# Uneven halves for dilated attention heads: 96 and 48 positions of a residue instead of 72 and 72

## The chip, the cores and the metric

The kernel runs on one core of one Trainium2 chip. The metric is device time in microseconds of one execution, the median of several runs. The core's engines are PE (matrix multiplication), DVE (vector), ACT (scalar and exponentials), POOL, and SP, which here issues the DMAs.

## The reference

Sliding-window attention feeds a two-layer feed-forward network (FFN) with GELU. Half of the heads have a plain window of 32 positions, the other half a window of 32 positions taken four apart (dilated). All data is float32.

```python
batch, n_heads, seq, head_dim = 8, 8, 576, 64
window, dilation = 32, 4
scores = q @ k.T / sqrt(64)
rel = pos[:, None] - pos[None, :]
mask_plain = (rel >= 0) & (rel < window)                                   # heads 0..3
mask_dil = (rel >= 0) & (rel < window * dilation) & (rel % dilation == 0)  # heads 4..7
attn = softmax(where(mask, scores, -1e9))
x = (attn @ v), heads side by side, reshaped to (8 * 576, 512)
h = x @ w_in                       # 512 -> 2048
out = gelu(h) @ w_out              # 2048 -> 512
```

A dilated query sees only keys whose position leaves the same remainder on division by 4. So a dilated head is four separate sequences ("residues") of 576 / 4 = 144 positions, each with a plain window of 32.

## The kernel before, in words

**Halves.** The 8 batches of 576 positions are cut into 16 half sequences `c` of 288 positions: `c = 2 * batch + half`. The FFN of one half works on tiles of 128 x 288. The eight heads are four pairs `p`: pairs 0 and 1 are plain, pairs 2 and 3 dilated.

**Blocks.** Attention is computed in blocks of 32 queries against 64 keys (the block's own 32 and the 32 before). In a dilated pair a half has 4 residues of 72 positions, so each residue needs three blocks `u`: two full ones and one with 8 positions. The four residues lie side by side on the 128 partitions (32 each). In a plain pair the nine blocks of a half are spread over the four partition groups, with the ninth alone.

**Steps of one pair.**
- `load` brings q and k (`raw_qk`) by DMA, issued by SP; `all_v` brings v for the four pairs.
- `scores` (line 310): for each block, each residue and each of two heads one matmul of 64 x 32 by 64 x 64 into PSUM.
- `lowest` (line 322): DVE adds the mask and finds the minimum of the negated scores; `softmax` (line 331): ACT's exponential with the sum, one for each block and head.
- `norm` (lines 352 to 361) and `turn` (lines 371 and 376): DVE divides by the sum and transposes the probabilities.
- `av` (line 411): for each block, residue and head one matmul of 64 x 64 by 64 x 32 (by 64 x 8 in a dilated third block) into PSUM tile `px_a`. A float32 matmul is two instructions in the trace, as with the scores.
- `xout` (lines 431 and 434): ACT rounds the result to `xh`, DVE subtracts to get the remainder `xl`. Both feed the FFN. For a dilated pair the store is strided, since positions of the four residues alternate.

**FFN.** Each product is made of three products of rounded parts (high x high, low x high, high x low). `ffn_h` (line 445) makes 12 matmuls for each of 16 tiles `f` of the hidden layer, ACT and DVE make `g` out of it, `ffn_o` (line 459) makes 12 more for each `f`.

**Order.** The halves 0 to 2 and the conversion of the weights are put in order by a planner, class `Plan`: a greedy list scheduler with a cost for each step, ranks, and rings of buffers that a job takes and gives back. The ring `wo` has 18 slots: weights as loaded (`raw_w`, and for some a shifted copy `mid_w`), q, k and v of halves 0 and 1, and the 16 finished `wout` tiles, which stay. The ring `raw` has 5 slots: `raw_qk` from half 2 on, and `cv`, a temporary of the weight conversion. From half 3 on the order is written out by hand: the attention of half `c` is woven into the FFN of half `c - 1`, which has positions 0 to 31 (16 for `ffn_h`, 16 for `ffn_o`).

```python
A_LOAD, A_V, A_SC, A_X = -6, 2, (3, 3, 9, 9), (22.5, 22.5, 27, 27)
```

So the dilated pairs' scores come at position 9, their `av` and `xout` at 27, and the loads six positions before the FFN of half `c - 1` begins.

Of the kernel before, what the change touches and what calls it, by code (L numbers as in the profile page):

```python
# [7 lines left out]
F32 = mybir.dt.float32  # L8
# [6 lines left out]
B, H, S, D = 8, 8, 576, 64  # L15
WIN, DIL = 32, 4
DM, DFF = H * D, 2048
P = 128
HALF = S // 2
NCH = B * 2  # L20
NPAIR = H // 2
NF = DFF // P
NC = DM // P
KW = HALF + WIN
QD = HALF // DIL

KB, NU = 32, 3
QP = HALF // 3  # L30
KD = QD + KB
NKMAX = 3 * KD + (NU + 1) * KB
NEG = -1.0e30
SCALE = 1.0 / 8.0
# [97 lines left out]


@with_exitstack
def attn_ffn(ctx: ExitStack, tc: tile.TileContext, qk_p, qk_d, v_p0, v_d0, v_p, v_d, w_in, w_out, outT):
    nc = tc.nc
    const = ctx.enter_context(tc.tile_pool(name="const", bufs=1))
    wpool = ctx.enter_context(tc.tile_pool(name="wpool", bufs=1))
    wo = ctx.enter_context(tc.tile_pool(name="wo", bufs=NF + 2))
    gpool = ctx.enter_context(tc.tile_pool(name="gpool", bufs=NF + 2))  # L140
    xpool = ctx.enter_context(tc.tile_pool(name="xpool", bufs=NC))
    work = ctx.enter_context(tc.tile_pool(name="work", bufs=2))
# [5 lines left out]
    def upper_banks(name, bufs):  # L148

        upper.close()  # L150
        return upper.enter_context(tc.tile_pool(name=name, bufs=bufs, space=bass.MemoryType.PSUM))
# [17 lines left out]
    select(DILATED0, ANY, None, -KB, 1, 0, ALU.is_ge)  # L169

    pools = dict(px=upper_banks("ps_x", 1))
    wins = [wpool.tile([P, 2, DM], F32R, name=f"win{f}") for f in range(NF)]
    wouts = [None] * NF

# [65 lines left out]
    def new_pair(c, p):  # L240
        s = Pair()
        s.c, s.p = c, p
        s.plain = p < NPAIR // 2
        k = p if s.plain else p - NPAIR // 2
        s.nr, s.nq = (3, QP) if s.plain else (DIL, QD)
        s.across = s.plain and c > 2
        if s.across:
            s.nr, s.nine = 4, 2 * (p % 2)
        s.rows = 32 * s.nr
        s.n = HALF + (KW if s.plain else NKMAX)  # L250
        s.src = (qk_p if s.plain else qk_d)[c, k]
        s.vsrc = (v_p0 if s.plain else v_d0)[c, k] if c < 2 else (v_p if s.plain else v_d)[c - 2, k]
        return s

    def load(s):

        yield {"DMA": 1.0 if s.plain else 1.2}
        if s.c < 2:
            s.raw = wo.tile([P, HALF + NKMAX], F32, tag="wo", name="raw_qk")
        else:  # L260
            s.raw = work.tile([P, HALF + NKMAX], F32, tag="raw", name="raw_qk", bufs=5)
        nc.sync.dma_start(s.raw[:, 0:s.n], s.src)

    def load_v(s):
# [13 lines left out]
    def groups(s, u):  # L278
        return range(s.nine, s.nine + 1) if s.across and u == NU - 1 else range(s.nr)

    def rows_of(s, u):
        g = groups(s, u)
        return slice(32 * g[0], 32 * g[-1] + 32)

    def parts(s):

        return [(rows_of(s, 0), 0, 2), (rows_of(s, 2), 2, 3)] if s.across else [(slice(0, s.rows), 0, NU)]

    def mask_of(s, u):
        k = ANY if s.c % 2 or u else PLAIN0 if s.plain else DILATED0  # L290
# [2 lines left out]
    def scores(s, banks=None):  # L293

        yield {"PE": 0.75}
        if banks is None:
            s.sc = [ps_m.tile([P, 512], F32, tag="m", name="ps_sc")[:, 0:2 * KB * NU] for _ in range(2)]
        else:
            s.sc = [banks[:, h, s.p % 2 * 2 * KB * NU:(s.p % 2 + 1) * 2 * KB * NU] for h in range(2)]
        for u in range(NU):  # L300
            for r in groups(s, u):
                if s.across:
                    q0 = (4 * u + r if u < 2 else 8) * KB
                    k0 = HALF + q0
                else:
                    q0 = r * s.nq + u * KB
                    k0 = HALF + r * (QP if s.plain else KD) + u * KB
                for h in range(2):
                    x = s.raw[h * D:(h + 1) * D]
                    nc.tensor.matmul(s.sc[h][32 * r:32 * r + 32, u * 2 * KB:(u + 1) * 2 * KB], x[:, q0:q0 + 32],  # L310
                                     x[:, k0:k0 + 2 * KB], start=True, stop=True)
# [67 lines left out]
    def av(s, banks=None):  # L379

        yield {"PE": (1.0 if s.plain else 1.3) if s.c < 2 else 0.9}
        n = s.nq
        if s.c < 2:
            px = pools["px"].tile([P, 4, 512], F32, tag="px", name="px")
            s.px = [(px[:, 0:s.nr, 0:n], 0, s.nr)]

            for m in (1, 3, 0, 2):
                i0, k = (2 * (m - 1) * 2 + 1, 2) if 0 < m < NU else (0, 1) if m == 0 else (4 * (NU - 1) + 1, 1)
                q0 = max(m - 1, 0) * KB
                for r in range(s.nr):  # L390
                    rows = slice(32 * r, 32 * r + 32)
                    t = s.t[rows].rearrange("p i j b -> p (i j) b")
                    for h in range(2):
                        i = i0 + 2 * h
                        nc.tensor.matmul(px[h * D:(h + 1) * D, r, q0:q0 + k * KB], s.v[rows, m, h * D:(h + 1) * D],  # L395
                                         t[:, i:i + 3 * k - 2:3], start=m == 1, stop=m == 2)
            return
        if banks is None:
            px = [ps_m.tile([P, 512], F32, tag="m", name="px2").rearrange("p (a n) -> p a n", a=2) for _ in range(2)]
            s.px = [(px[0][:, :, 0:n], 0, 2), (px[1][:, 0:s.nr - 2, 0:n], 2, s.nr)]  # L400
        else:
            at = s.p % 2 * QP
            s.px = [(banks.rearrange("p k (a n) -> p (k a) n", a=2)[:, 0:s.nr, at:at + n], 0, s.nr)]
        for u in range(NU):
            b = min(KB, n - u * KB)
            for j in range(2):
                for r in sorted((r for r in groups(s, u) if r % 2 == j), reverse=s.across and s.nine > 0):
                    px, r0, _ = s.px[-1] if r >= s.px[-1][1] else s.px[0]
                    rows = slice(r // 2 * 64, r // 2 * 64 + 64)
                    for h in range(2):  # L410
                        nc.tensor.matmul(px[h * D:(h + 1) * D, r - r0, u * KB:u * KB + b],  # L411
                                         s.v[rows, u, j, h * D:(h + 1) * D], s.t[rows, 2 * u + h, j, 0:b],
                                         start=True, stop=True)

    def xout(s):
        for i, (px, r0, r1) in enumerate(s.px):
            yield {"ACT": 0.46 if len(s.px) == 1 else 0.34}
            if i == 0:
                if s.c == 1:
                    s.x = s.of["x"][:, s.p, 0], s.of["x"][:, s.p, 1]  # L420
                else:
                    s.x = tuple(xpool.tile([P, HALF], F32R, tag=n, name=n) for n in ("xh", "xl"))
            if s.across:
                two = [x[:, 0:8 * KB].rearrange("p (u r b) -> p r u b", u=2, r=4) for x in s.x]
                put = [(px[:, :, 0:2 * KB].rearrange("p r (u b) -> p r u b", u=2), two),
                       (px[:, s.nine, 2 * KB:], [x[:, 8 * KB:] for x in s.x])]
            else:
                put = [(px, [x.rearrange("p (r i) -> p r i" if s.plain else "p (i r) -> p r i", r=s.nr)[:, r0:r1]
                             for x in s.x])]
            for y, (h, l) in put:  # L430
                nc.scalar.copy(h, y)  # L431
            yield {"DVE": 0.48 if len(s.px) == 1 else 0.3}
            for y, (h, l) in put:
                nc.vector.tensor_sub(l, y, h)  # L434
# [66 lines left out]
    def attention_jobs(plan, c, prev, gate):  # L501

        for p in range(NPAIR):
            s, k, rank = xs[c][p], (c, p), R_ATT[c] + R_P * p

            def add(name, gen, after, take=(), give=(), delay=0.15):
                plan.add((name,) + k, gen, after, take, give, rank + R_A[name], delay)
            last, ring = [] if prev is None else [prev], "wo" if c < 2 else "raw"
            add("load", load(s), [("begun", ("load",) + j) for j in last], [ring], delay=2.2)
            v = ("v",) + k if c < 2 else ("v", c)  # L510
            if c < 2:
# [28 lines left out]
            prev = k  # L540
# [22 lines left out]
    k = attention_jobs(plan, 0, None, [])  # L563
    k = attention_jobs(plan, 1, k, [])
# [54 lines left out]
    for c in range(3, NCH):  # L619
        def add(at, rank, gen, c=c):  # L620
            steps.append((2 * NF * (c - 1) + at, rank, len(steps), gen))
        add(A_V, 0, all_v(c))
        for p, s in enumerate(xs[c]):
            add(A_LOAD, 0, load(s))
            add(A_SC[p], 1, scores_of(s))
            for u in range(NU):
                add(A_SC[p], 2, lowest(s, u))
                add(A_E[p], 3, softmax(s, u))
            add(A_N[p], 4, norm(s))
            add(A_N[p], 5, turn(s))  # L630
            add(A_X[p], 6, av_of(s))
            add(A_X[p], 7, xout(s))
# [98 lines left out]
```

## Time and profile before

| | us |
|---|---|
| timed runs | 948.16, 945.34, 947.63 |
| median of the three | 947.63 |
| profiled execution, its own time | 945.82 |
| span of its trace, first to last instruction | 944.0 |
| PE busy in the span | 916.4 (97%) |
| DVE busy | 500.2 (53%) |
| ACT busy | 435.4 (46%) |
| POOL busy | 21.0 (2%) |

PE and PEld are two rows of one engine: matmuls, and the loads of their stationary operand, which overlap them. The ends of matmuls are modelled in the trace, their starts are recorded. "L445" is line 445 of the kernel. In the chain of work that ended last, each piece is a stretch of one engine's work that the next piece waited for or followed.

### The profile page before, as it was taken

To read this page: it belongs to the slowest core of one execution; us is meant where nothing else is said; L and a number is where in the kernel's file an instruction comes from. 1 tells how busy PE (TensorE), PEld (TensorE's weight loads), DVE (VectorE), ACT (ScalarE), POOL (GpSimd) and SP (SyncE) were. 2 spreads that over 40 slices of the span, in tenths; PEclk is the share of its full clock that TensorE was granted. 3 is DMA by queue.
4 is the path that set the end of the run, shared out by engine and by line. 5 is a ranking of instruction groups with operands and counts; after the bars stand their busy time and mean duration, and the time that the engine had idled before them with its cause. 6 is when DMAs were issued, how large, how long until landed. Compare 5 with 4: busy or idle time off the path is not lost.

```text
span 944.0 us, 27638 instructions
## 1 busy us (share of the span) xinstructions
PE 916.4 (97%) x11632; PEld 898.6 (95%) x11632; DVE 500.2 (53%) x1957; ACT 435.4 (46%) x1398; POOL 21.0 (2%) x64
## 2 busy tenths in 40 slices
PE   4599999999999999999999999999999999999998
PEld 3499999999999999999999999999999999999998
DVE  6889974364635446354454635446354454635420
ACT  5535453634536245363634546255363634546240
POOL 1400020000000000000000000000000000000000
PEclk9999999999999999999999999999999999999999
DMA  9987233022040401204022040401204022040000
GB/s 319 405 297 261 92 126 137 4 78 75 8 145 8 132 17 51 103 8 145 2 82 71 8 146 8 138 9 60 93 8 145 2 86 68 13 139 8 21 1 26
DMA packets 34988, 83.69 MB, mean 89 GB/s; under 512 B 3888, under 2 KB 12080, under 8 KB 34864
## 3 DMA queue, kind: packets, MB, share of 16 engines
q1 hardware_dynamic: 34864, 81.93, 25.3%
q8 instruction: 91, 1.49, 0.7%
q14 instruction: 33, 0.27, 0.1%
HBM read 72.47 MB, written 9.44 MB: 87 GB/s over the span
## 4 chain that ended last, share of the span: by engine, by line
PE 96%; DMA 1%; issue 1%; DVE 1%; ACT 0%; SPq 0%
PE ps_h L445 44%; PE ps_o L459 44%; PE px_a L411 4%; PE ps_a L310 3%; DMA raw_qk<-qk_d 1%; PE px L395 1%; PE ps_sc L310 1%; DMA raw_w<-w_in 0%; DVE sm L322 0%; PE px L411 0%; DVE cv L199 0%; DVE sm L361 0%; ACT sm L331 0%; DVE cv L197 0%; DVE win L232 0%
## 5 line engine op out<-in xcount | busy, mean ns | idle before, releaser
L459 PE MATMUL ps_o<-g,wout 128*128 128x288 f32 x3072 | 420.1, 296 | 0.0
L459 PEld LDWEIGHTS ps_o<-g,wout 128*128 128x128 f32 x3072 | 409.7, 188 | 0.9
L445 PE MATMUL ps_h<-xh,win 128*128 128x288 f32 x1920 | 388.7, 297 | 0.0
L445 PEld LDWEIGHTS ps_h<-xh,win 128*128 128x128 f32 x1920 | 308.2, 188 | 2.8
L445 PE MATMUL ps_h<-xl,win 128*128 128x288 f32 x960 | 284.0, 296 | 0.0
L454 DVE TENSOR_TENSOR g<-gf,g 128x288 fp32r<-128x288 f32 x256 | 117.0, 457 | 259.2 <-ACT g L452 259.0
L449 ACT ACTIVATE gf<-ps_h 128x288 f32<-128x288 f32 x256 | 105.2, 411 | 297.6 <-PE ps_h L445 297.5
L445 PEld LDWEIGHTS ps_h<-xl,win 128*128 128x128 f32 x960 | 181.0, 189 | 0.0
L331 ACT ACTIVATE sm<-sm,st 128x64 f32<-128x64 f32 (+1 forms) x360 | 120.2, 335 | 12.5 <-DVE st L322 11.4
L452 ACT CAST g<-gf 128x288 fp32r<-128x288 f32 x256 | 111.0, 434 | 7.9
L431 ACT CAST xh<-px_a 128x256 fp32r<-128x256 f32 (+1 forms) x78 | 29.5, 413 | 132.7 <-PE px_a L411 84.8
L376 DVE STREAM_TRANSPOSE turned<-sm 32x192 f32<-32x192 f32 (+2 forms) x248 | 81.3, 328 | 6.2
L179 DVE COPY o_sb<-ps_o 128x288 f32<-128x288 f32 x58 | 26.4, 456 | 83.3 <-PE ps_o L459 82.4
L331 ACT ACTIVATION_READ_ACCUMULATOR sm<-sm,st 128x1 f32 (+1 forms) x360 | 67.2, 187 | 0.0
L434 DVE TENSOR_TENSOR xl<-px_a,xh 128x256 fp32r<-128x256 f32 (+1 forms) x78 | 31.3, 429 | 37.5 <-ACT xh L431 37.1
L322 DVE CUSTOM_DVE_ANT_0 sm<-ps_a,masks 128x64 f32<-128x64 f32 (+1 forms) x312 | 48.0, 216 | 0.6
L371 DVE STREAM_TRANSPOSE turned<-sm 128x256 f32<-128x256 f32 (+2 forms) x90 | 41.1, 457 | 9.0 <-POOL sm L358 4.2
L411 PEld LDWEIGHTS px_a<-turned,v_all 64*64 64x64 f32 x2184 | 35.6, 135 | 4.3 <-issue 4.3
L411 PE MATMUL px_a<-turned,v_all 64*64 64x32 f32 (+1 forms) x2184 | 38.2, 216 | 0.0
L361 DVE TENSOR_TENSOR sm<-sm,st 128x256 f32<-128x256 f32 (+2 forms) x82 | 35.1, 428 | 2.8
L352 DVE TENSOR_SCALAR st<-st 128x4 f32<-128x4 f32 (+2 forms) x90 | 14.2, 160 | 31.0 <-ACT sm L331 30.1
L310 PE MATMUL ps_sc<-raw_qk 64*32 64x64 f32 x504 | 12.3, 294 | 18.8 <-issue 8.4
(40 smaller groups left out, 392.8 us busy)
## 6 DMA issues: line engine op xcount, KB each, us to landing
raw_qk<-qk_d SPq DMA_DIRECT2D x32, 364.0 KB, 5.4
v_all<-v_p SPq DMA_DIRECT2D x28, 384.0 KB, 3.8
v_all<-v_d SPq DMA_DIRECT2D x28, 384.0 KB, 5.4
raw_qk<-qk_p SPq DMA_DIRECT2D x32, 304.0 KB, 4.2
outT<-o_sb SPq DMA_DIRECT2D x64, 144.0 KB, 1.8
raw_w<-w_in SPq DMA_DIRECT2D x16, 512.0 KB, 6.1
raw_w<-w_out SPq DMA_DIRECT2D x16, 512.0 KB, 5.7
mid_w<-w_out SPq DMA_DIRECT2D x10, 511.5 KB, 8.0
```

What stands on the lines that cost most here:

```text
L310: nc.tensor.matmul(s.sc[h][32 * r:32 * r + 32, u * 2 * KB:(u + 1) * 2 * KB], x[:, q0:q0 + 32], x[:, k0:k0 + 2 * KB], start=True, stop=True)
L322: nc.vector.tensor_tensor_reduce(out=s.sm[rs, i], in0=s.sc[h][rs, cols], in1=mask_of(s, u), scale=-SCALE, scalar=3.0e38, op0=ALU.add, op1= ...
L331: nc.scalar.activation(t, t, AF.Exp, bias=s.st[rs, 0, i:i + 1], scale=-1.0, accum_out=s.st[rs, 1, i:i + 1])
L361: nc.vector.tensor_mul(t, t, st.unsqueeze(2).broadcast_to((rs.stop - rs.start, 2 * (u1 - u0), 2 * KB)))
L371: nc.vector.transpose(s.t[rs, i].rearrange("p i j b -> p (i j b)"), s.sm[rs, i].rearrange("p i k -> p (i k)"))
L376: nc.vector.transpose(s.t[32 * to:32 * to + 32, i, r % 2], s.sm[32 * r:32 * r + 32, i, j * KB:(j + 1) * KB])
L411: nc.tensor.matmul(px[h * D:(h + 1) * D, r - r0, u * KB:u * KB + b], s.v[rows, u, j, h * D:(h + 1) * D], s.t[rows, 2 * u + h, j, 0:b], sta ...
L445: nc.tensor.matmul(ps, wins[f][:, t, cc * P:(cc + 1) * P], xx, start=(n == 0), stop=(n == 3 * NC - 1))
L449: nc.scalar.activation(gf, ps, AF.Gelu)
L452: nc.scalar.copy(g[:, 0], gf)
L454: nc.vector.tensor_sub(g[:, 1], gf, g[:, 0])
L459: nc.tensor.matmul(ps, wouts[f][:, t, d * P:(d + 1) * P], gs[f][:, u], start=(f == 0 and n == 0), stop=(f == NF - 1 and n == 2))
```

## The change

For batches 2 to 7 (halves 4 to 15), the dilated pairs are no longer cut 72 + 72. In the even half of a batch each residue takes 96 positions, three full blocks; in the odd half 48, two blocks (32 and 16). Per batch and pair, five blocks stand where six stood.

The FFN still works on 288 positions a half. So an even half computes 24 positions of each residue that belong to the next half: ACT copies them out of PSUM into a new tile `kept` (128 x 4 x 24, one for each dilated pair), and in the odd half they are the first 24 of each residue in `xh` and `xl`, beside the 48 computed there.

The inputs `qk_w` and `qk_r` are new arrays with q and k in the new cut; v of these halves is packed anew. Because q and k of an even half now need 768 columns, the tiles of dilated pairs come from the ring `wo` (1024 columns each), from half 2 on, and the tiles of the ring `raw` shrink from 728 columns to 608. For half 2 this is a change of ring in the planner too.

```diff
+QW = NU * KB
+QR = 2 * QD - QW
...
+    kept = [const.tile([P, DIL, QW - QD], F32, name=f"kept{k}") for k in range(NPAIR // 2)]
...
+        s.nk = QP if s.plain else KD
+        s.split = not s.plain and c > 3
+        s.src = (qk_p if s.plain else qk_d)[min(c, 3) if s.split else c, k]
+        if s.split:
+            s.nq, s.nk = (QR, QR + KB) if c % 2 else (QW, QW)
+            s.n = (DIL * (s.nq + s.nk) + KB) if c % 2 else 2 * DIL * QW
+            s.src = (qk_r if c % 2 else qk_w)[c // 2 - 2, k]
+            s.kept = kept[k]
+        s.nu = -(-s.nq // KB) if not s.across else NU
...
-        if s.c < 2:
-            s.raw = wo.tile([P, HALF + NKMAX], F32, tag="wo", name="raw_qk")
+        if s.c < 2 or not s.plain:
+            s.raw = wo.tile([P, 2 * DM], F32, tag="wo", name="raw_qk")
         else:
-            s.raw = work.tile([P, HALF + NKMAX], F32, tag="raw", name="raw_qk", bufs=5)
+            s.raw = work.tile([P, HALF + KW], F32, tag="raw", name="raw_qk", bufs=5)
...
-        for u in range(NU):                      # in scores, av and the hand-written order
+        for u in range(s.nu):
...
+                elif s.split:
+                    q0 = r * s.nq + u * KB
+                    k0 = DIL * s.nq + r * s.nk + (u - (s.c % 2 == 0)) * KB
...
+            elif s.split:
+                xs_ = [x.rearrange("p (i r) -> p r i", r=DIL) for x in s.x]
+                if s.c % 2:
+                    put = [(s.kept, [x[:, :, 0:QD - QR] for x in xs_]), (px, [x[:, :, QD - QR:] for x in xs_])]
+                else:
+                    put = [(px[:, :, 0:QD], xs_)]
+                    nc.scalar.copy(s.kept, px[:, :, QD:])
...
-            last, ring = [] if prev is None else [prev], "wo" if c < 2 else "raw"
+            last, ring = [] if prev is None else [prev], "raw" if c == 2 and s.plain else "wo"
```

More of the change, by code (lines that the diff above doesn't have):

```diff
@@ L134, in attn_ffn @@
 @with_exitstack
-def attn_ffn(ctx: ExitStack, tc: tile.TileContext, qk_p, qk_d, v_p0, v_d0, v_p, v_d, w_in, w_out, outT):
+def attn_ffn(ctx: ExitStack, tc: tile.TileContext, qk_p, qk_d, qk_w, qk_r, v_p0, v_d0, v_p, v_d, w_in, w_out, outT):
     nc = tc.nc
@@ L250, in new_pair @@
         s.n = HALF + (KW if s.plain else NKMAX)
-        s.src = (qk_p if s.plain else qk_d)[c, k]
+        s.nk = QP if s.plain else KD
[7 more added lines that the diff above has]
+        s.nu = -(-s.nq // KB) if not s.across else NU
         s.vsrc = (v_p0 if s.plain else v_d0)[c, k] if c < 2 else (v_p if s.plain else v_d)[c - 2, k]
@@ L285, in parts @@
     def parts(s):
-        return [(rows_of(s, 0), 0, 2), (rows_of(s, 2), 2, 3)] if s.across else [(slice(0, s.rows), 0, NU)]
+        return [(rows_of(s, 0), 0, 2), (rows_of(s, 2), 2, 3)] if s.across else [(slice(0, s.rows), 0, s.nu)]
     def mask_of(s, u):
@@ L304, in scores @@
                     k0 = HALF + q0
+                elif s.split:
+                    q0 = r * s.nq + u * KB
+                    k0 = DIL * s.nq + r * s.nk + (u - (s.c % 2 == 0)) * KB
                 else:
                     q0 = r * s.nq + u * KB
-                    k0 = HALF + r * (QP if s.plain else KD) + u * KB
+                    k0 = HALF + r * s.nk + u * KB
                 for h in range(2):
@@ L403, in av @@
             s.px = [(banks.rearrange("p k (a n) -> p (k a) n", a=2)[:, 0:s.nr, at:at + n], 0, s.nr)]
-        for u in range(NU):
+        for u in range(s.nu):
             b = min(KB, n - u * KB)
@@ L625, in attn_ffn @@
             add(A_SC[p], 1, scores_of(s))
-            for u in range(NU):
+            for u in range(s.nu):
                 add(A_SC[p], 2, lowest(s, u))
@@ L713 @@
     vd0, vd = keys_down(np.stack([vr[..., t * QD:t * QD + KD, :] for t in range(2)], 1), DIL)
-    vd = by_halves(vd)
+    vsplit = np.zeros((B - 2, 2, hp // 2, 2, DIL, NU + 1, KB, D), v.dtype)
+    vr2 = vr[2:].reshape(B - 2, hp // 2, 2, DIL, S // DIL + KB, D)
+    vsplit[:, 0].reshape(B - 2, hp // 2, 2, DIL, -1, D)[:] = vr2[..., :QW + KB, :]
+    vsplit[:, 1].reshape(B - 2, hp // 2, 2, DIL, -1, D)[..., :QR + KB, :] = vr2[..., QW:, :]
+    vsplit = vsplit.reshape((NCH - 4,) + vsplit.shape[2:])
+    vd[2:] = np.stack([vsplit[..., :NU, :, :], vsplit[..., 1:, :, :]], 5)
+    vd = by_halves(vd)
+    qk_w = np.concatenate([heads_first(qr[2:, ..., :QW, :].reshape(B - 2, hp // 2, 2, DIL * QW, D)),
+                           heads_first(kr[2:, ..., KB:KB + QW, :].reshape(B - 2, hp // 2, 2, DIL * QW, D))], -1)
+    qk_r = np.concatenate([heads_first(qr[2:, ..., QW:, :].reshape(B - 2, hp // 2, 2, DIL * QR, D)),
+                           heads_first(kr[2:, ..., QW:, :].reshape(B - 2, hp // 2, 2, DIL * (QR + KB), D)),
+                           np.zeros((B - 2, hp // 2, 2 * D, KB), q.dtype)], -1)
     wi = np.asarray(inputs["moe_w_in"]).view(np.int64).reshape(NC, P, NF, P).transpose(2, 1, 0, 3).reshape(NF, P, DM)
@@ L720 @@
     arrays, args = {}, []
-    for name, a in (("qk_p", qk_p), ("qk_d", qk_d), ("v_p0", vp0), ("v_d0", vd0), ("v_p", vp), ("v_d", vd), ("w_in", wi),
+    for name, a in (("qk_p", qk_p), ("qk_d", qk_d), ("qk_w", qk_w), ("qk_r", qk_r), ("v_p0", vp0), ("v_d0", vd0), ("v_p", vp), ("v_d", vd), ("w_in", wi),
                     ("w_out", wo)):
```

## The prediction

> **What bounds the kernel now.** I read three views in this order: the page's busy times, the stretches table, and the chain that ended last.
>
> ```profile
> PE 916.4 (97%) x11632; PEld 898.6 (95%) x11632; DVE 500.2 (53%) x1957; ACT 435.4 (46%) x1398; POOL 21.0 (2%) x64
> ...
> 36.00:53.00 17.00, 12.69 (x351) 10.99 (x344) 14.42 (x64) 7.65 (x14) 2.69 (x6) 0.90 0.98 389
> 53.00:71.60 18.60, 18.60 (x145) 18.59 (x141) 17.98 (x53) 8.31 (x18) 0.00 (x0) 1.00 0.82 278
> ...
> 267.81:324.36 56.55, 56.55 (x722) 55.66 (x722) 27.80 (x116) 26.63 (x88) 0.00 (x0) 1.00 0.19 64
> ```
>
> The columns of a stretch are its length, then busy time of PE, weight load, DVE, ACT and POOL, the granted clock and the DMA share. From 53 us on PE is never idle. In one steady period (the FFN of one half sequence, with the attention of the next half woven in) it works 56.55 of 56.55 us, DVE 27.80, ACT 26.63, DMA 0.19. So there, a PE microsecond removed is a microsecond of the end, and the other engines have half of each period to spare. The chain shows the start of the first such period, what PE does in the third, and the last half, which has no attention woven in:
>
> ```profile
> 154.66 6.37 PE ps_h L445 x48
> ...
> 267.81 6.37 PE ps_h L445 x48
> 274.18 0.93 PE ps_a L310 x60
> 275.10 9.75 PE ps_h L445 x72
> 284.86 1.13 PE ps_a L310 x73
> 285.98 9.76 PE ps_h L445 x72
> 295.74 10.74 PE ps_o L459 x81
> 306.48 1.26 PE px_a L411 x72
> 307.74 7.37 PE ps_o L459 x54
> 315.11 1.51 PE px_a L411 x96
> ...
> 889.80 25.49 PE ps_h L445 x192
> 915.29 25.40 PE ps_o L459 x192
> ```
>
> The bare FFN is 25.49 + 25.40 = 50.89 us, so the attention of a half costs 56.55 - 50.89 = 5.66 us of PE. Plain scores are the 0.93, dilated scores the 1.13, plain probabilities times v ("AV") the 1.26, dilated AV the 1.51; the remaining 0.83 is spent around these pieces. This period carries the attention of half 5, an odd half of the third batch: the first whose third block the change drops.
>
> **The change part by part.**
>
> *PE, AV.* In halves 5, 7, ... 15 (six of them) block u=2 of both dilated pairs disappears: 4 residues x 2 heads = 8 matmuls per pair, each two instructions in the trace. Three narrow looks at PE give the first instruction of each block (of half 4, whose stream has the same shape):
>
> ```profile
> 258.46 0.26 PE L411 MATMUL px_a<-turned,v_all 64*64 64x32 f32 x4
> 258.95 0.39 PE L411 MATMUL px_a<-turned,v_all 64*64 64x8 f32 x15
> 259.18 0.39 PE L411 MATMUL px_a<-turned,v_all 64*64 64x32 f32 x13
> 259.65 0.39 PE L411 MATMUL px_a<-turned,v_all 64*64 64x8 f32 x15
> 259.97 0.40 PE L459 MATMUL ps_o<-g,wout 128*128 128x288 f32 x1
> ...
> L411 PE MATMUL px_a<-turned,v_all 64*64 64x32 f32 x1768 | 34.7, 221 | 0.0
> ...
> L411 PE MATMUL px_a<-turned,v_all 64*64 64x8 f32 x416 | 10.2, 199 | 0.0
> ```
>
> The first number of the first five is the start; the last two are the same two forms in the list of groups, mean 221 and 199 ns an instruction from its start to a modelled end. Two blocks of 32 columns take 258.95 - 258.46 = 0.49 us, then 259.65 - 259.18 = 0.47: 0.235 to 0.245 a block. The block of 8 columns takes 259.18 - 258.95 = 0.23. A block costs the same with 8 or 32 columns. So dropping it in an odd half saves 2 x 0.235 = 0.47 us; the second block shrinking from 32 to 16 columns saves nothing; and the third block of an even half growing from 8 to 32 columns costs 0 to 0.01 each, which I take as nothing. Floor for this term: dilated 96 instructions in 1.51 against plain 72 in 1.26 gives 0.25/24 = 10.4 ns each, x 32 = 0.33. Ceiling: a third of 1.51 = 0.50. I take 0.47, the direct reading.
>
> The Trainium skill, page "TensorE: Matmul & The Clock Gate", section "What happens when you issue a matmul", says that matmul throughput is purely N cycles, one column a cycle. By that, the columns would count, 72 + 72 before and 96 + 48 after, AV would save nothing and the sum below would be 2.2 instead of 5.0; the starts above (0.23 for 8 columns, 0.235 to 0.245 for 32) speak against it at this width.
>
> *PE, scores.* The same block u=2 goes: 2 pairs x 8 matmuls x 2 = 32 of 96 instructions.
>
> ```profile
> 284.78:285.05 0.27, 0.27 (x32) 0.27 (x33) 0.00 (x0) 1.00 0.00 0
> 285.05:285.77 0.72, 0.72 (x92) 0.72 (x68) 0.00 (x0) 1.00 0.00 0
> ```
>
> These are stretches of the score instructions alone (columns as before, without ACT). The first 32 start within 0.27 us, a burst; the other 64 (the 92 includes those still running) start over 0.72, 11.2 ns each. What goes comes out of the slow part: 32 x 11.2 = 0.36 us. Floor: 1.13 - 0.93 over 24 instructions is 8.3 ns, x 32 = 0.27. Ceiling: 1.13/3 = 0.38. I take 0.36.
>
> *Sum on PE:* 6 x (0.47 + 0.36) = 5.0 us; ends 6 x (0.33 + 0.27) = 3.6 and 6 x (0.50 + 0.38) = 5.3.
>
> *ACT and DVE.* An odd half loses four exponentials and four minimum passes; the even half gains one ACT copy of 128x96 per pair into `kept`; the odd half's evacuation becomes two ACT casts and two DVE subtractions per pair (96 and 192 elements) where there was one each.
>
> ```profile
> L331 ACT ACTIVATE sm<-sm,st 128x64 f32<-128x64 f32 (+1 forms) x360 | 120.2, 335 | 12.5 <-DVE st L322 11.4
> ...
> L331 ACT ACTIVATION_READ_ACCUMULATOR sm<-sm,st 128x1 f32 (+1 forms) x360 | 67.2, 187 | 0.0
> ...
> L431 ACT CAST xh<-px 128x144 fp32r<-128x144 f32 x4 | 1.4, 444 | 3.9 <-PE px L411 3.9
> ...
> 260.11 0.68 ACT L431 CAST xh<-px_a 128x288 fp32r<-128x288 f32 x1 [5.03 <-PE px_a L411]
> ...
> 262.24 0.69 DVE L434 TENSOR_TENSOR xl<-px_a,xh 128x288 fp32r<-128x288 f32 x1 [0.74 <-ACT xh L431]
> ```
>
> The removed work is 4 x (0.335 + 0.187) = 2.1 us of ACT per odd half. The added: a strided cast costs 0.68 at 288 elements and 0.444 at 144, so 1.6 ns an element and about 0.21 fixed; splitting one in two adds about 0.21 us on ACT and, with DVE's cast-sized subtraction alike, 0.21 there, per pair; an even half's copy of 96 is at most 0.21 + 96 x 1.6 ns = 0.37. All of it lies on the path from AV to the next FFN: AV ends at 259.97, the last subtraction at 262.24 + 0.69 = 262.93, and the FFN that reads it starts one period before 324.36, at 267.81. That leaves 4.88 us; an even half needs 2 x 0.37 = 0.74 of it, an odd one 2 x 0.42 = 0.84 (less what AV now ends earlier, 0.47). Without this cover six even halves and six odd ones would cost 6 x 0.74 + 6 x 0.84 = 9.5 us; with it, nothing. `kept` is written a whole period before it is read.
>
> *DMA and the queue of SP.* q and k of an even dilated pair become 768 columns (393 KB, was 364), of an odd one 544 (279 KB): less in sum, at a DMA share of 0.19. These loads now use the `wo` ring: 18 slots, 16 kept by `wout`, two left, which the scores of the half before must release. Dilated scores end at 285.98; the next loads are issued here:
>
> ```profile
> 317.33 0.86 SPq L262 DMA_DIRECT2D raw_qk<-qk_d  x2
> ```
>
> That is 31 us later, so nothing behind them on SP waits. Cost nothing; if a slot were late, the stores behind would be too.
>
> *The start.* Half 2's two dilated loads also move from `raw` to `wo`, while weights still stream through `wo`. The planner's order may shift.
>
> ```profile
> 24.44 2.00 SPq L262 DMA_DIRECT2D raw_qk<-qk_d  x2
> 51.55 0.85 PE L310 MATMUL ps_sc<-raw_qk 64*32 64x64 f32 x43
> ...
> L185 SPq DMA_DIRECT2D raw_w<-w_in x5: 327/328/422, 1.2 to 32.3; - x5
> L185 SPq DMA_DIRECT2D raw_w<-w_out x5: 327/328/1494, 5.2 to 34.7; - x5
> ...
> L216 DVE TENSOR_SCALAR raw_w<-mid_w x4: 382/398/428, 18.7 to 34.6; 128x512 uint32<-128x512 uint32 x4
> ...
> L220 DVE TENSOR_SCALAR raw_w<-raw_w x1: 428/428/428, 5.2 to 5.2; 128x512 uint32<-128x512 uint32 x1
> ...
> 20.86 0.43 DVE L216 TENSOR_SCALAR raw_w<-mid_w 128x512 uint32<-128x512 uint32 x1 [1.45 <-DMA mid_w<-w_in]
> ...
> DVE raw_w L220 <- DMA raw_w<-w_in: 5.2, 1, 5.2
> DVE raw_w L216 <- DMA mid_w<-w_in: 1.4, 1, 1.4
> ```
>
> Two of 18 slots are held from 24.4 to the scores at 51.6. The middle rows are the tile `raw_w` up to 34.8 us (count; durations; first and last start): SP has issued ten weights (5 + 5), DVE has begun five (4 + 1), so five lie ahead. DVE's only waits for a weight are the last two rows, once each, at 5.2 and at 20.86. Losing one weight of depth costs nothing by that. In exchange `raw`, where half 2 held four of five slots and the conversions' `cv` had one, gets two back: at best the DVE idle time of the stretch 36 to 53, 17.00 - 14.42 = 2.6 us, is regained. I take 0, since no wait for a weight follows 21 us; the ends are -2.6 and, if the stretch's PE idle time of 17.00 - 12.69 = 4.3 us doubles, +4.3.
>
> **Sum.** The profiled execution took 945.82 (span 944.0 and 1.82 around it): 945.82 - 5.0 = 940.8. The three timed runs have median 947.63, 1.81 above the profiled one; the mean of all four is 946.7, and 946.7 - 5.0 = 941.7, which I predict. A change under 0.3%, 2.8 us, cannot be told from none here; 5.0 is 0.53%.
>
> **The rivals.**
> 1. *PE time goes by columns:* AV saves nothing, the wide third block of an even half takes back what the odd one gives, and only the scores are left, 6 x 0.36 = 2.2: 946.7 - 2.2 = 944.5. For it: the 8-column form is shorter in the list, 199 against 221 ns. Against: the starts, which don't rest on modelled ends. Chance 0.09. This is the Trainium skill's rule quoted above.
> 2. *The start gains too,* from the freed `raw` slots: 941.7 - 2.6 = 939.1. For it: half 2 holds four of five slots for some 27 us. Against: DMA is at 0.98 there, so weights come no sooner. Chance 0.09.
> 3. *The start loses as much as the rest gains:* the slots held in `wo` starve the weights, PE idles. With one of five weights of lead lost over 27 us and the lead the limit, 27/5 = 5.4 us: 947.1, no change. Against: those two wait rows. Chance 0.06.
> 4. *Slower:* the planner, with other free times in both rings, sets a pair of weights later than now, in the stretch before 53 us. PE then lacks the FFN step that this pair feeds: 12 matmuls, of which 192 take 25.49, so 1.6 us, and four such steps (both stages of two halves) 6.4. One pair set back that far gives 941.7 + 6.4 = 948.1, no change; two give 954.5. It decides from 5.0 + 2.8 = 7.8 us late, more than one pair. Against: the five weights of lead. Chance 0.04.
> 5. *The longer evacuation stalls the FFN:* all 9.5 us come back, 951.2. Against: 4.88 us of cover. Under 0.01, counted with 4.
>
> **How the numbers follow.** The forecast has 0.72. Its own range is 946.7 - 5.3 = 941.4 to 946.7 - 3.6 = 943.1, and the runs' spread, (948.16 - 945.34)/2 = 1.4, to each side. Down to 938.5 it takes in most of rival 2, up to 945.5 all of rival 1; 3, 4 and 5 stay out, with 0.1. Faster by over 0.3%: forecast and rival 2, 0.81. Within: 1 and 3, 0.15. Slower: 0.04.
>
> **What the next profile would show.** Right: six periods (attention of halves 5, 7, ... 15) near 55.7 and seven near 56.55; dilated score pieces of 0.77 and AV pieces of 1.04 in odd halves, 1.13 and 1.51 in even ones; FFN matmuls after AV with no idle time; the first steady period starting at 154.7. Wrong: even halves whose AV piece grows to 2.0 (columns count); a steady start before 152 or after 157 (the planner); PE idle before L445 with ACT or DVE named (evacuation); an L262 wait on SP with stores behind it.

## The result and the profile after

| | before, us | after, us |
|---|---|---|
| median | 946.08 (6 runs, 944.92 to 948.16) | 940.79 (6 runs, 939.79 to 942.91) |
| profiled execution | 945.82 | 942.59 |
| span of its trace | 944.0 | 940.8 |

The ratio is 0.9946, 95% interval 0.9927 to 0.9964: 5.1 us of 946 less. The forecast, 941.7 out of 946.7, is a ratio of 0.9947.

The line numbers after: `ps_h` is L470 (was 445), `ps_o` L484 (459), `px_a` L429 (411), `ps_a` L328 (310), `xh` L456 and `xl` L459 (431, 434). First the row of busy times, then the table of stretches with the same columns as before: two of the start, one period with the attention of an even half (212.83 to 269.39) and one of an odd half.

```profile
PE 914.6 (97%) x11248; PEld 896.5 (95%) x11248; DVE 491.5 (52%) x1921; ACT 429.7 (46%) x1374; POOL 20.9 (2%) x64
...
36.00:53.00 17.00, 13.35 (x345) 11.63 (x343) 12.96 (x60) 7.29 (x13) 2.25 (x6) 0.81 0.88 342
53.00:71.60 18.60, 18.60 (x131) 18.60 (x129) 17.09 (x50) 7.45 (x16) 0.00 (x0) 0.90 0.86 287
...
212.83:269.39 56.56, 56.56 (x723) 55.64 (x722) 27.79 (x116) 26.92 (x90) 0.00 (x0) 1.00 0.18 61
269.39:325.10 55.71, 55.71 (x659) 54.80 (x658) 26.36 (x110) 25.40 (x82) 0.00 (x0) 1.00 0.20 66
```

PE is still busy for the whole of both periods; the odd period has 64 matmul instructions less (723 to 659) and is 0.85 us shorter; the even one is what it was. The chain of that odd period, the dilated AV of the next even half, and the last half:

```profile
156.25 6.37 PE ps_h L470 x48
...
269.39 6.37 PE ps_h L470 x48
275.76 0.91 PE ps_a L328 x60
276.67 9.75 PE ps_h L470 x72
286.42 0.79 PE ps_a L328 x53
287.21 9.76 PE ps_h L470 x72
296.97 10.71 PE ps_o L484 x81
307.68 1.31 PE px_a L429 x72
308.98 7.33 PE ps_o L484 x54
316.32 1.05 PE px_a L429 x64
...
372.41 1.53 PE px_a L429 x96
...
886.59 25.49 PE ps_h L470 x192
```

Only two pieces differ by more than 0.05: dilated scores 0.79 for 1.13, dilated AV 1.05 for 1.51. From the first steady period to the last half it is 886.59 - 156.25 = 730.34, before 889.80 - 154.66 = 735.14: 4.80 less. The steady part began 156.25 - 154.66 = 1.59 later in this execution, which is why the two profiled spans differ by only 3.2 (the timed medians differ by 5.3); of this start more below.

### The profile page after: what moved, and what is told of

Same layout as the page of the kernel before. It is cut to its first block, busy times and chain, and to the rows that moved or that the text cites. A ratio compares the mean times of both kernels' runs of the same rounds, so it can differ in the third digit from the quotient of the medians.

```text
span 940.8 us, 26805 instructions
## 1 busy us (share of the span) xinstructions
PE 914.6 (97%) x11248; PEld 896.5 (95%) x11248; DVE 491.5 (52%) x1921; ACT 429.7 (46%) x1374; POOL 20.9 (2%) x64
## 4 chain that ended last, share of the span: by engine, by line
PE 96%; DMA 2%; issue 1%; DVE 1%; SPq 0%; ACT 0%; DVEq 0%
PE ps_h L470 44%; PE ps_o L484 44%; PE px_a L429 4%; PE ps_a L328 3%; DMA mid_w<-w_in 1%; DMA raw_qk<-qk_d 1%; PE px L413 1%; PE ps_sc L328 0%; PE px L429 0%; ACT sm L349 0%; SPq L283 0%; SPq L276 0%; DVE cv L205 0%; DVE sm L340 0%; DVE xl L459 0%
## 5 line engine op out<-in xcount | busy, mean ns | idle before, releaser
L484 PE MATMUL ps_o<-g,wout 128*128 128x288 f32 x3072 | 420.3, 296 | 0.0
L484 PEld LDWEIGHTS ps_o<-g,wout 128*128 128x128 f32 x3072 | 409.9, 188 | 1.1
L470 PE MATMUL ps_h<-xh,win 128*128 128x288 f32 x1920 | 390.6, 299 | 0.0
L470 PEld LDWEIGHTS ps_h<-xh,win 128*128 128x128 f32 x1920 | 309.9, 190 | 2.9 <-issue 0.3
L470 PE MATMUL ps_h<-xl,win 128*128 128x288 f32 x960 | 285.1, 297 | 0.0
L470 PEld LDWEIGHTS ps_h<-xl,win 128*128 128x128 f32 x960 | 182.1, 190 | 0.0
L349 ACT ACTIVATE sm<-sm,st 128x64 f32<-128x64 f32 (+2 forms) x336 | 112.2, 335 | 11.5 <-DVE st L340 10.4
L394 DVE STREAM_TRANSPOSE turned<-sm 32x128 f32<-32x128 f32 (+2 forms) x248 | 78.1, 315 | 6.2
L456 ACT CAST xh<-px_a 128x256 fp32r<-128x256 f32 (+2 forms) x78 | 27.5, 387 | 99.5 <-PE px_a L429 61.4
L349 ACT ACTIVATION_READ_ACCUMULATOR sm<-sm,st 128x1 f32 (+2 forms) x336 | 62.7, 186 | 0.0
L459 DVE TENSOR_TENSOR xl<-px_a,xh 128x256 fp32r<-128x256 f32 (+2 forms) x78 | 29.0, 399 | 37.4 <-ACT xh L456 37.0
L340 DVE CUSTOM_DVE_ANT_0 sm<-ps_a,masks 128x64 f32<-128x64 f32 (+1 forms) x288 | 44.5, 216 | 0.6
L429 PEld LDWEIGHTS px_a<-turned,v_all 64*64 64x64 f32 x1992 | 32.7, 135 | 4.2 <-issue 4.2
L429 PE MATMUL px_a<-turned,v_all 64*64 64x32 f32 (+2 forms) x1992 | 35.5, 219 | 0.0
L328 PE MATMUL ps_sc<-raw_qk 64*32 64x64 f32 x504 | 12.4, 300 | 17.1 <-issue 7.5
```

The source lines that it names most:

```text
L340: nc.vector.tensor_tensor_reduce(out=s.sm[rs, i], in0=s.sc[h][rs, cols], in1=mask_of(s, u), scale=-SCALE, scalar=3.0e38, op0=ALU.add, op1= ...
L349: nc.scalar.activation(t, t, AF.Exp, bias=s.st[rs, 0, i:i + 1], scale=-1.0, accum_out=s.st[rs, 1, i:i + 1])
L394: nc.vector.transpose(s.t[32 * to:32 * to + 32, i, r % 2], s.sm[32 * r:32 * r + 32, i, j * KB:(j + 1) * KB])
L470: nc.tensor.matmul(ps, wins[f][:, t, cc * P:(cc + 1) * P], xx, start=(n == 0), stop=(n == 3 * NC - 1))
L484: nc.tensor.matmul(ps, wouts[f][:, t, d * P:(d + 1) * P], gs[f][:, u], start=(f == 0 and n == 0), stop=(f == NF - 1 and n == 2))
```

## The experiments

Each ratio is to the kernel before, from the runs of the same chip.

**1. The dropped score block put back (`redo_scores`).**

```diff
-        for u in range(s.nu):
+        for u, at in [(u, u) for u in range(s.nu)] + [(1, 2)] * (s.nu < NU):
...   (block 1 once more, into the columns of block 2)
```

> The changed kernel, but in the odd halves 5 to 15 the second score block of a dilated pair is computed once more, into the columns of PSUM where the third block used to lie (nobody reads them). Instruction count on PE as before the change for the scores, everything else as after. Theory (the gain is PE instructions that are gone, at their rate in the stream): the dilated score piece of an odd half goes back from 0.79 to 1.13 us, its period from 55.70 to 56.04, and 6 x 0.34 = 2.0 of the 5.1 us are lost: ratio to the kernel before 0.9967. Rival (the gain lies in the lighter ACT and DVE work or in the start): the time stays at the changed kernel's, ratio 0.9946.

**2. The dropped AV block put back, at 16 columns (`redo_av`).**

```diff
-        for u in range(s.nu):
+        for u in list(range(s.nu)) + [1] * (s.nu < NU):
```

> The changed kernel, but in the odd halves the second block of probabilities times v (16 columns) is computed twice, the second time over the first. Theory: the dilated AV piece of an odd half goes back from 1.05 to 1.51 us although these are blocks of 16 columns, its period to 56.16, and 6 x 0.46 = 2.8 us are lost: ratio 0.9976. Rival (PE time goes by columns): 16 of 48 columns more, a third of 1.05, 0.35 an odd half, 2.1 us: ratio 0.9968. Rival (gain elsewhere): 0.9946.

The dilated pieces of an odd half in the chain, scores and AV, of the first and then of the second kernel:

```profile
397.23 1.13 PE ps_a L328 x73
...
427.46 1.05 PE px_a L429 x64
```

```profile
399.81 0.79 PE ps_a L328 x53
...
429.73 1.52 PE px_a L429 x96
```

Each block brings its piece back to the length before the change and leaves the other. Timed, `redo_scores` gives 0.9962 (0.9949 to 0.9976) where 0.9967 was expected, `redo_av` 0.9972 (0.9962 to 0.9983) where 0.9976 was. They give back 1.5 and 2.5 of the 5.1 us; their pieces say 6 x 0.34 = 2.0 and 6 x 0.47 = 2.8, within the intervals' 1.2 us or so. That the saving lies in the lighter ACT and DVE work or at the start would leave 0.9946, which is under both intervals; but the change's own interval reaches 0.9964, so the ratios alone do not decide it. The periods do, as the chain's starts give them: with the score block back the odd ones of halves 5 to 15 take 56.03 to 56.08 (56.04 expected, 55.70 to 55.77 without it), with the AV block back 56.17 to 56.24 (56.16 expected), and the even ones stay at 56.50 to 56.57. The 0.47 of the AV block also speaks against a price by columns (0.35), which its ratio can't tell apart.

**3. The rings alone (`ring_only`).**

```diff
-        if s.c < 2:
+        if s.c < 2 or not s.plain:
...
-            last, ring = [] if prev is None else [prev], "wo" if c < 2 else "raw"
+            last, ring = [] if prev is None else [prev], "raw" if c == 2 and s.plain else "wo"
```

> The kernel before, with the change of rings alone: dilated q and k from half 2 on in the ring wo, tiles of the ring raw cut to 608 columns; halves stay 72 + 72. Theory (rings cost and gain nothing; the later steady start in the profile of the changed kernel, 156.25 against 154.66, is three half-clock windows instead of one): ratio 1.000 within 0.0015, all periods 56.55, and a steady start near 154.7 when the profile has one half-clock window. Rival (the freed raw slots help the start): 2.6 us less, ratio 0.9973. Rival (the held wo slots hurt): 1.6 us more, 1.0017, and a start of 156 at one half-clock window.

0.9992 (0.9984 to 1.0001): between 1.5 us won and 0.1 lost. Neither the 2.6 won nor the 1.6 lost is there. How a profile's steady part comes to start early or late is seen in the chain, in the first group of 24 FFN matmuls (behind it PE has no pause) and in the first steady period. The group in the kernel before and in the changed kernel:

```profile
53.08 3.40 PE ps_h L445 x24
```

```profile
53.04 5.03 PE ps_h L470 x24
```

Group and steady start in this kernel, then in `redo_scores` and `redo_av`, each of the latter two with its span and mean granted clock:

```profile
53.53 3.40 PE ps_h L445 x24
...
155.07 6.37 PE ps_h L445 x48
```

```profile
52.94 3.41 PE ps_h L470 x24
...
154.58 6.37 PE ps_h L470 x48
...
core 0: 940.8 us, clock 0.998
```

```profile
55.41 3.38 PE ps_h L470 x24
...
156.99 6.37 PE ps_h L470 x48
...
core 0: 944.2 us, clock 0.998
```

From the end of the group to the steady start it is 98.1 to 98.2 us in all five kernels, so the start is decided up to there, and in two ways. In the changed kernel the group begins as early as before (53.04 and 53.08) but takes 5.03 - 3.40 = 1.63 us more: this is the start that came 1.59 later. The granted clock of the stretch 53.00 to 71.60 was 0.90 there and 1.00 before, as the expectation's half-clock windows have it; with the same rings this kernel's group takes 3.40. `redo_scores` and `redo_av` differ only in what they do from half 5 on, and their groups are equally fast; yet PE comes to the group 2.47 later in the second, with the same rings. So a single profile's start says nothing of the rings. Why PE comes to the group later in one execution, and where the lower clock falls, stays open.

**4. The third block at 32 columns (`wide32`) and every dilated block at 64 (`wide64`).** Both start from the kernel before. In `wide64` a matmul of an odd residue streams its neighbour's probabilities ahead of its own, so its values for these residues are not the attention's.

```diff
-            b = min(KB, n - u * KB)
+            b = min(KB, n - u * KB) if banks is None else KB          # wide32
...
+                        if wide:                                       # wide64
+                            t = s.t[rows, 2 * u + h].rearrange("p j b -> p (j b)")
```

> The kernel before, but from half 3 on the third AV block of a dilated pair runs with 32 columns instead of 8 (the extra columns fall into unused PSUM). Theory (a block costs the same with 8 or 32 columns): periods stay at 56.55 to 56.6, ratio 1.000. Rival (columns count, 72 columns in 1.51 us): 13 x 2 x 24 columns more, the AV piece 1.51 x 96/72 = 2.0, 13 x 0.5 = 6.5 us slower, ratio 1.0069.

> The kernel before, but from half 3 on every AV block of a dilated pair streams 64 columns (the block's probabilities and those of its neighbour; the extra columns are overwritten or unused). Theory (a wave of four instructions starts every 58 ns whatever the columns, up to some width): if 64 columns still fit, the dilated AV piece stays at 1.51. Rival (the 58 ns are the time of 32 float32 columns and the 8-column block is at the same floor by chance): it doubles to 3.0, periods 58.0.

The dilated AV piece in the chain, of `wide32` and then of `wide64`:

```profile
428.36 1.53 PE px_a L413 x96
```

```profile
260.15 1.56 PE px_a L417 x96
```

`wide32`: 0.9998 (0.9989 to 1.0008), against 1.0069 by columns. With a third block of 8 columns the piece is 1.51, of 32 columns 1.53, with all blocks of 64 columns 1.56. A residue's columns grow from 72 to 96 and to 192, the piece by 1% and 3%: at these widths a block has a fixed price, about 0.23 us. In `wide64` the six blocks start 0.233 us apart (260.185 to 261.352), as those of 8 and 32 columns did by the prediction's rows (0.23 to 0.25). `wide64` ran once and its time is not compared; the claim rests on its piece.

**5. How much the evacuation may grow (`evac30`).**

```diff
-                    nc.scalar.copy(s.kept, px[:, :, QD:])
+                    for _ in range(31):
+                        nc.scalar.copy(s.kept, px[:, :, QD:])
```

> The changed kernel with 30 more copies into kept in each even half and dilated pair, ahead of the casts (results unchanged). In the changed kernel two such copies start 0.14 us apart, so this is 2 x 30 x 0.14 = 8.4 us more on ACT between AV and the next FFN. Cover by its profile: the last subtraction ends at 264.79, the FFN starts at 269.39 and comes to the fourth pair's remainder 1.5 later, 6.1 in all. Theory: 8.4 - 6.1 = 2.3 us of PE idle in each of six even halves, 14 us: ratio 0.9946 + 0.0148 = 1.009, idle time before L470 with DVE xl named. Rival (the evacuation is already the limit, the cover is less): up to 6 x 8.4 = 50 us, ratio 1.048. Rival (it is hidden altogether by other slack): 0.9946.

The ratio was 1.0718 (1.0703 to 1.0733), over the 1.009 expected and over the 1.048 of the worst rival. Instructions of ACT, then of PE at the next FFN, in order of time:

```profile
261.35 8.36 ACT L452 COPY kept<-px_a 128x96 f32<-128x96 f32 x31 [5.02 <-PE px_a L429]
...
271.00 8.34 ACT L452 COPY kept<-px_a 128x96 f32<-128x96 f32 x31 [0.73 <-DVE xl L460]
...
270.32 0.53 PE L471 MATMUL ps_h<-xh,win 128*128 128x288 f32 x2 [0.48 <-ACT xh L457]
271.03 0.40 PE L471 MATMUL ps_h<-xl,win 128*128 128x288 f32 x1 [0.17 <-DVE xl L460]
279.97 0.85 PE L471 MATMUL ps_h<-xh,win 128*128 128x288 f32 x2 [8.54 <-ACT xh L457]
...
268.00:281.00 13.00, 3.80 (x20) 2.91 (x20) 1.72 (x4) 11.10 (x41) 0.00 (x0) 0.69 0.00 0
```

Two sizes were missed. A copy takes 8.36/31 = 0.27 us in a row, not the 0.14 between two starts of different instructions, so with one copy at 0.24 us in the changed kernel 2 x (8.35 - 0.24) = 16.2 us were added and not 8.4. PE was idle 0.48 + 0.17 + 8.54 = 9.2 of them: the cover is 16.2 - 9.2 = 7.0 us, near the 6.1 that the profile gave. The wait named is mostly that for ACT's cast `xh`, where DVE's `xl` was expected: the copies stand ahead of that cast. And the loss of (1.0718 - 0.9946) x 946 / 6 = 12.2 us an even half is 3.0 more than the idle time: the granted clock is 0.69 in the last row's stretch, and the first FFN matmuls after the gap run slower (two take 0.85 us at 279.97 and 0.53 at 270.32). So the change's evacuation, up to 0.8 us longer by the prediction, lies well inside the cover, and beyond the cover the loss here was 12.2 us for 9.2 of waiting.

**6. One piece instead of two, for AV (`one_av`) and for scores (`one_sc`).** These look for the 0.83 us around the four pieces.

```diff
-    A_LOAD, A_V, A_SC, A_X = -6, 2, (3, 3, 9, 9), (22.5, 22.5, 27, 27)
+    A_LOAD, A_V, A_SC, A_X = -6, 2, (3, 3, 9, 9), (27, 27, 27, 27)        # one_av
+    A_LOAD, A_V, A_SC, A_X = -6, 2, (9, 9, 9, 9), (22.5, 22.5, 27, 27)    # one_sc
```

> The changed kernel with AV of all four pairs at position 27 of the hand-written order, instead of the plain pairs at 22.5 and the dilated ones at 27. The four attention pieces of a period cost 56.55 - 50.89 = 5.66 us, of which 0.83 lies around the pieces, 0.21 each. Theory (each change between FFN and attention matmuls has its own price): one piece less saves 0.21 x 13 = 2.7 us, ratio 0.9946 - 0.0029 = 0.9917, as the evacuation of four pairs (about 5.5 us) still fits before the next FFN. Rival (the evacuation is then late): PE idle before L470 in every period, no gain or a loss. Rival (the price belongs to the instructions, not to the change): 0.9946.

> The changed kernel with the scores of all four pairs at position 9. Theory of a price for each change of pieces: 2.7 us less, ratio 0.9917. Rival (the burst at the head of a score piece, 32 instructions in 0.27 us against 11.2 ns each after it, is worth about as much): 32 x (11.2 - 8.3) = 0.09 lost per period, a gain of 1.5 left, 0.9930; with the slower rate for the whole burst, none, 0.9946.

No gain over the change's 0.9946: 0.9943 (0.9929 to 0.9957) and 0.9947 (0.9934 to 0.9961). But not for the reason of either rival alone. Chain, PE's order of time and a stretch of `one_av`:

```profile
296.33 17.85 PE ps_o L484 x135
314.17 2.10 PE px_a L429 x136
...
705.09 2.41 PE L429 MATMUL px_a<-turned,v_all 64*64 64x32 f32 x150
708.88 0.85 PE L429 MATMUL px_a<-turned,v_all 64*64 64x32 f32 x18 [1.38 <-issue]
...
700.00:719.96 19.96, 18.58 (x265) 18.24 (x265) 8.24 (x21) 3.84 (x9) 0.00 (x0) 0.83 0.23 76
```

The merged piece of an odd half takes 2.10 for 1.31 + 1.05 = 2.36, and with what lies around it that period was 324.06 - 268.75 = 55.31, 0.40 less than 55.71. Another period lost about as much as all of them won, 60.75 us for 56.59: in the merged piece of an even half (150 + 18 = 168 instructions) PE waited 1.38 us for nothing that a semaphore explains, and the clock granted was 0.83 over the stretch. `one_sc` shows such a gap too, with the DMA activity of that time; there the clock stayed at 1.00 behind it (233.40 to 237.00):

```profile
229.47 1.96 PE L328 MATMUL ps_a<-raw_qk 64*32 64x64 f32 x167
233.41 0.24 PE L328 MATMUL ps_a<-raw_qk 64*32 64x64 f32 x1 [1.98 <-issue]
...
DMA packets 2, 0.03 MB, mean 4 GB/s; under 512 B 0, under 2 KB 0, under 8 KB 0
## 3 DMA queue, kind: packets, MB, share of 16 engines
q8 instruction: 2, 0.03, 1.6%
```

All that moves between 226 and 235 us are two packets of the queue that brings instructions. The piece's last matmul comes 1.98 us late with all data at hand. The reading that fits is that PE ran out of fetched instructions, since 168 matmuls and as many weight loads were to go in some 2 us. The Trainium skill, page "Runtime: NRT & Kernel Launch", section "Instruction fetch mechanics", says that instructions are refilled in blocks of 16 KiB (256 instructions) and that crossing a block is mostly hidden. The packet size agrees (0.03 MB for two), and the 336 instructions of the piece would be 1.3 blocks; hidden the crossing is not in a piece this dense. The traces point further the same way. In PE's records in order of start (matmuls, weight loads and semaphore instructions), the five gaps of this kind over 0.5 us, 0.79 and 1.38 in `one_av`, 1.98 and 1.16 in `one_sc` and 0.73 in `odd_one` below, stand behind records 10689, 17601, 5825, 19649 and 10689, each 193 more than a multiple of 256. The 256 records before a gap had started within 1.3 to 3.5 us; in the changed kernel's steady part no 256 between two such places take less than 5.47, and none ends in a gap. Not every quick 256 ends in one: in `split1_odd` PE went on behind 256 that had taken 1.96 us. So the gaps stand where one block of 256 would end and the next begin. That the fetch is the cause is inferred from this; no run changed the fetch alone.

**7. Merged in odd halves only (`odd_one`), the uneven cut from the second batch on (`split1`), and both (`split1_odd`).**

```diff
+        if c > 3:                                                          # odd_one
+            A_SC, A_X = ((9, 9, 9, 9), (27, 27, 27, 27)) if c % 2 else ((3, 3, 9, 9), (22.5, 22.5, 27, 27))
...
-        s.split = not s.plain and c > 3
+        s.split = not s.plain and c > 1                                    # split1
```

> The changed kernel with all four pairs' scores at position 9 and all AV at 27, but in odd halves 5 to 15 alone, where the change leaves 136 instead of 168 instructions in such a merged piece. In the two runs that merged everywhere, odd periods without a stall were 55.31 (AV merged) and 55.42 (scores merged) against 55.70, and the merged kernels' gaps of PE that no semaphore explains stood mostly in even ones. Theory (PE runs out of fetched instructions in a long piece of small matmuls, and shorter merged pieces mostly escape): odd periods near 55.0, 6 x 0.7 = 4.2 us less than the changed kernel, ratio 0.9946 - 0.0044 = 0.990, with at most one or two such gaps, which would take 1 to 4 us back, 0.992 to 0.994. Rival (the gaps come with any merging): 0.9946 or more.

> The changed kernel with the uneven cut from the second batch on (halves 2 and 3 too; half 2 is in the planner's part). Theory (0.85 us of PE for each odd half whose third block goes): the period with the attention of half 3 becomes 55.70, ratio 0.9946 - 0.0009 = 0.9937; too small to be told by the ratio, to be read from the period. Rival (the planner's part pays for it): a steady start more than 1 us later at equal clock.

> Both of these: uneven cut from half 2 on, pieces merged in odd halves 3 to 15. Theory: 7 x 0.7 + 0.85 = 5.8 us less than the changed kernel if no instruction gap falls in, ratio 0.9885; with gaps up to 0.993. If it stays under the changed kernel's interval it is the fastest of these versions.

`odd_one` 0.9914 (0.9902 to 0.9927), `split1` 0.9931 (0.9918 to 0.9945), `split1_odd` 0.9891 (0.9878 to 0.9905), median 935.31. The last interval ends under the lower end of the change's, 0.9927, so this version is faster than the change; its ratio is the lowest here, but its interval still touches that of `odd_one`. One of its odd periods in the chain:

```profile
267.90 15.93 PE ps_h L470 x120
283.83 1.58 PE ps_a L328 x97
285.41 9.75 PE ps_h L470 x72
295.17 17.88 PE ps_o L484 x135
313.04 2.10 PE px_a L429 x136
315.14 7.73 PE ps_o L484 x57
322.88 2.13 PE ps_h L470 x16
```

The period is 322.88 - 267.90 = 54.98, against 55.71 with four pieces: 0.73, where 0.7 was expected, and here 136 matmuls a piece run without a gap. `odd_one` had one in its six odd periods, 13 FFN matmuls behind a merged AV piece:

```profile
431.38 1.89 PE L484 MATMUL ps_o<-g,wout 128*128 128x288 f32 x12 [0.73 <-issue]
```

`split1` by itself can't be told from the change by its interval, as expected. Its period with the attention of half 3 is 210.34 - 154.59 = 55.75, where 55.70 was expected, and its steady start of 154.59 is no later than the 154.66 before, at the same mean clock of 0.998: the rival's loss in the planner's part is not in this profile.

## Why the prediction was right, point by point

- *What bounds:* right. Both periods show PE busy for their whole length, and putting the PE blocks back brought the time back, with ACT and DVE left as light as the change made them.
- *AV, 0.47 an odd half:* measured 1.51 - 1.05 = 0.46. A block costs nearly the same at 8, 16, 32 and 64 columns; the wider third block of an even half costs 0.02 (1.53), where 0 to 0.01 was allowed and nothing taken, 0.1 us in all.
- *Scores, 0.36:* measured 1.13 - 0.79 = 0.34, between the floor of 0.27 and the value taken.
- *The sum of 5.0:* the steady part is 4.80 shorter in the two traces; the timed ratio gives 5.1. The mechanism is right; that the ratio agrees to 0.0001 is partly luck, since its interval leaves about 1.8 us to either side.
- *Evacuation and `kept`, nothing:* right. The last subtraction of an even half ends at 264.12 + 0.67 = 264.79, by the first row, with the FFN starting at 269.39; that of an odd half ends at 319.03 + 0.51 = 319.54, by the second, with the FFN at 325.10:

```profile
264.12 0.67 DVE L459 TENSOR_TENSOR xl<-px_a,xh 128x288 fp32r<-128x288 f32 x1 [0.89 <-ACT xh L456]
...
319.03 0.51 DVE L459 TENSOR_TENSOR xl<-px_a,xh 128x192 fp32r<-128x192 f32 x1 [0.32 <-ACT xh L456]
```

  That is 4.60 and 5.56 of cover left, of 4.88 before.
- *SP and the ring in the steady part, nothing:* right; no PE wait in the steady part names a load. (The prediction's 393 and 279 KB for q and k are in other units than its 364; in the page's units they are 384 and 272, still less in sum.)
- *The start, 0 between -2.6 and +4.3:* `ring_only` bounds the rings' share between -1.5 and +0.1, and the timed ratio's 5.1 against the steady part's 4.80 leaves about 0 for the start. The changed kernel's profile has its steady start at 156.25, not at the 154.7 that was forecast: the 1.59 lie in the group of 24 FFN matmuls at a lower granted clock, by the rows above. PE's arrival at that group and the place of the lower clock differ from one execution to the next; the prediction had them only as the runs' spread.
- *The rivals:* columns fell with `wide32`; a gain or a loss at the start with `ring_only`; a stalled FFN with `evac30`, where 7.0 of 16.2 us added stayed hidden.

## What to carry to other kernels

When one engine is busy for the whole of a period, price the removed work from that engine's starts in that stretch: the starts gave 0.47 for a measured 0.46, where the mean durations (221 and 199 ns) make a narrow block look cheaper. Where small matmuls come in blocks of fixed price, as here, cut the work into fewer, fuller blocks; what is computed too early can wait in a small tile if the copies lie inside cover that the profile shows. Merging the four pieces of small matmuls into two saved 0.73 us in an odd period here, but only where no "issue" gap fell in: look for such gaps inside the merged piece and behind it.

## What the runs showed of the hardware that I had not expected

- A block of 16 small float32 matmul instructions of 64 x 64 takes about 0.23 us with 8 to 64 columns (pieces of 1.51, 1.53 and 1.56 for 96 instructions).
- 0.83 us of a period lie around its four attention pieces, about 0.2 each. Merging two pieces of a kind saved 0.40 a period for AV and 0.29 for scores; for AV 0.26 of it lies inside the piece (2.10 for 2.36). What the change between kinds of matmul costs by itself is not shown.
- A dense piece of 168 small matmuls and as many weight loads can stop for 1.2 to 2.0 us with nothing to wait for. With pieces of 136 PE stopped once in `one_av` (0.79) and once in `odd_one` (0.73), shortly behind the piece, and not at all in `split1_odd`. All five gaps stand at the same place of a count by 256 instructions.
- An idle gap of 1.38 us was followed by a granted clock of 0.83 over 20 us, and its period took 4.2 us more; behind a gap of 1.98 us the clock stayed at 1.00. So a short gap can come with a slower clock, and what decides it is not shown.
